# One attention and two MLP layers on one core: layer 1's first tokens loaded during attention, two of its buffers in space of their own, three buffers for raw weights

## The chip, the cores and the metric

The kernel runs on one core of a Trainium2 chip. The metric is device microseconds of one execution; the median of three runs of the kernel before is 1123.8 us (1122.57 to 1123.87). The engines are named as in the profile: PE is TensorE (PEld its weight loads), DVE VectorE, ACT ScalarE, POOL GpSimd, SP the queue that issues all DMAs here.

## The reference

Attention with a threshold (scores more than tau below the row's maximum are dropped), then two MLP layers, all in float32:

```python
scores = q @ k.T * scale                       # 4 batches, 8 heads, 576 tokens, head width 64
scores = where(scores >= max - tau, scores, -1e9)
x  = softmax(scores) @ v                       # gathered to 2304 tokens x 512
h  = x @ w_in1;  x = (h * sigmoid(1.702 * h)) @ w_out1      # 512 -> 2048 -> 512
h  = x @ w_in2;  out = (h * tanh(softplus(h))) @ w_out2     # 512 -> 2048 -> 512
```

The weights reach the kernel as 64-bit words of which the kernel makes float32 values itself (called conversion below), and every matrix product of the MLP layers is done in three passes, with each operand split in a high and a low part.

## The kernel before

Three stages follow each other on PE: attention, layer 1, layer 2. Activations pass between them through DRAM (`x_d`).

**Attention** runs over 80 groups (4 batches, 4 pairs of heads, 5 tiles of query rows). A group is: scores on PE (L586), the softmax on DVE (L605, L609, L615), ACT (L612) and POOL (L628), transposes on PE (L662) with copies on ACT (L672), the product with v on PE (L683), and a copy on ACT (L691). When a pair of heads is done its rows are stored to `x_d` (L693). Score banks and the four banks of `h` in layer 1 share PSUM: layer 1's first matmul must come after the last scores (`open_hb`).

**Layer 1** runs over five blocks of tokens (512, 256, 512, 512, 512) and, in each, over 16 slices `f` of the hidden width. `h1(j, f)` is 12 matmuls (L487), a tanh (L513, ACT), a product (L516, DVE), a copy to the high part `gh` (L518, ACT) and the difference `gl` (L519, DVE). `o1(j, f)` is 12 matmuls (L532) that accumulate the output; it comes two units behind, so that PE's order is h(n), o(n-2), h(n+1), and so on.

**Weights.** Slice `f` has 1 MB of raw words (two loads, L368 and L372) in a buffer of the ring `sr` (`NSR` buffers). `conv_w` makes a value of them in a buffer of the ring `sv` (three buffers): ACT L377 and L379, DVE L383 and L386, POOL L389, DVE L391. `split_w` makes the high part (ACT L397) and the low part (DVE L399) in the slice's own space. Slice f is allowed to start when group 60 + 4f has its softmax; from f=5 on that is the last group. Layer 2's weights are converted in layer 1's second block and after (`stage_w2`) and go through DRAM.

**Tokens.** `load_x(layer, j, rank)` brings a block's tokens in two halves: a load into an `sv` buffer (L468), a copy to the high part on ACT (L472), the difference on DVE (L474). Block 0 goes to `xa`, a tile that exists from the start. Rings hand out their buffers in the order in which the program calls them.

**Order.** Nothing is executed in the order of the text: `Order` keeps a list of operations with engine, duration, what they depend on and a rank, and a greedy planner at build time writes out each engine's queue. An engine that comes free takes the ready operation of lowest rank. A load is put down as 2.0 us and its bytes at 200e3 per us, one after the other (`DMA_US`, `DMA_RATE`). Operations with `port=True` (the conversion's on DVE and POOL, L474, L615, L628) are never planned at the same time on DVE and POOL. On the chip each queue then runs in that order, each instruction waiting for what it needs.

`opened` stands for the end of attention: only then `a`, attention's pool, is closed, and its space is used for weights 12 to 15, `x`, and layer 1's `t`, `gh`, `gl` and `x2`.

Of the kernel before, what the change touches and what calls it, by code (L numbers as in the profile page):

```python
# [22 lines left out]
PR = 2  # L23
AR = 0.1
NORM_P = 1.0
NSR = 2
NSV = 3
WARM = 1
FG = 0.2
# [14 lines left out]
C0 = 60  # L44
C1 = 4
D0 = 16
D1 = 2


class Order:  # L50
# [23 lines left out]
    def add(self, eng, dur, fn, r=(), w=(), rank=0.0, deps=(), nbytes=None, port=False, steps=1):  # L74
        n = len(self.ops)
        if port:
            self.port.add(n)
        before = set(deps)
        for key in r:
            if key in self.writer:  # L80
                before.add(self.writer[key])
        for key in w:
            if key in self.writer:
                before.add(self.writer[key])
            before.update(self.readers.get(key, ()))
        for key in r:
            self.readers.setdefault(key, []).append(n)
        for key in w:
            self.writer[key] = n
            self.readers[key] = []  # L90
        before.discard(n)
        self.ops.append((eng, dur, fn, before, rank, nbytes, steps))
        return n
# [106 lines left out]
def attention_then_two_ffn_kernel(  # L200
# [98 lines left out]
    def t_mm(n, k=1):  # L299
        return k * (max(n, 256) * 0.4167e-3 + 0.0125)  # L300

    def t_dve(n, fast=False):
        return 0.065 + n * (0.52e-3 if fast else 1.042e-3)

    def t_act(n, ptr=0, psum=True):
        return (0.05 if psum else 0.09) + n * 0.833e-3 + 0.093 * ptr
# [7 lines left out]
    def dma(fn, nbytes, r=(), w=(), rank=0.0, deps=(), dur=0.47):  # L314
        return add("SP", dur, fn, r, w, rank, deps, nbytes)
# [14 lines left out]
    spool = stage_ctx.enter_context(tc.tile_pool(name="s", bufs=1, side="right"))  # L330
    srs = Ring(spool, "sr", NSR, [128, 4 * DM], F32)
    svs = Ring(vpool, "sv", NSV, [128, 2 * DM], F32)
    W = []

    def make_w(pool, upto):
        for f in range(len(W), upto):
            W.append([pool.tile([128, 2 * DM], F32R, name=f"w{p}{f}") for p in "hl"])
# [64 lines left out]
    def load_w1(f, rank, deps):  # L402
        val, kval = conv_w(1, f, rank, deps)
        split_w(f, val, kval, rank)
# [9 lines left out]
    def load_w2(f, rank):  # L414
# [5 lines left out]
    late = {  # L420
        "x": LateRing("x", 1, [128, 2, KD, T], F32R),
        "o": LateRing("o", NOUT, [128, 512], F32),
        "x2": LateRing("x2", 4, [128, T], F32),
        "t": LateRing("t", 2, [128, T], F32),
        "gh": LateRing("gh", 3, [128, T], F32R),
        "gl": LateRing("gl", 3, [128, T], F32R),
        "m": LateRing("ms", 5, [128, T], F32),
        "hs": LateRing("hs", NHS, [128, T], F32),
        "g2h": LateRing("g2h", NG2, [128, T], F32R),
        "g2l": LateRing("g2l", NG2, [128, T], F32R),  # L430
    }

    def open_late(olds, new):

        def go():
            for old in olds:
                old.close()
            if len(W) < KF:
                make_w(ctx.enter_context(tc.tile_pool(name="wb", bufs=1)), KF)
            for where, name, rings, side in new:  # L440
                pool = where.enter_context(tc.tile_pool(name=name, bufs=1, side=side))
                for ring in rings:
                    late[ring].make(pool)

        return go
# [7 lines left out]
    def load_x(layer, j, rank):  # L453

        t0, n = blocks[layer][j]
        deps = [i for i, lay, a, b in x_stores if lay == layer and a < t0 + n and b > t0]
        x, kx = (lambda: x0), ("xa", 0)
        if x_n[0] % 2:
            x, kx = late["x"].next()
            deps.append(opened)  # L460
        x_n[0] += 1
        keys = []
        for i in range(2):
            rt, kr = svs.next()
            r = rt.rearrange("p (c t) -> p c t", c=2)[:, :, 0:n]
            cs = slice(2 * i, 2 * i + 2)
            kh, kl = kx + (0, i), kx + (1, i)
            dma(lambda r=r, cs=cs: nc.sync.dma_start(  # L468
                out=r, in_=x_d[layer][cs, :, t0:t0 + n].rearrange("c p t -> p c t")),
                256 * n * 4, [], [kr], rank, deps)  # L470
            add("ACT", t_act(2 * n, psum=False),
                lambda r=r, cs=cs: nc.scalar.copy(x()[:, 0, cs, 0:n], r), [kr], [kh], rank, deps)  # L472
            add("DVE", t_dve(2 * n),
                lambda r=r, cs=cs: nc.vector.tensor_tensor(  # L474
                    x()[:, 1, cs, 0:n], r, x()[:, 0, cs, 0:n], ALU.subtract),
                [kr, kh], [kl], rank, port=True)
            keys += [kh, kl]
        xt[layer, j] = (x, keys)

    def mm_h(dst, layer, j, f):  # L480
        n = blocks[layer][j][1]
        ih, il = (parts(w)[0] for w in W[f])
        x = xt[layer, j][0]()
        i = 0
        for c in range(KD):
            for a, lo in ((ih, 0), (ih, 1), (il, 0)):
                nc.tensor.matmul(  # L487
                    hb[dst][:, 0:n], a[:, c, :], x[:, lo, c, 0:n], start=(i == 0), stop=(i == 3 * KD - 1))
                i += 1
                yield  # L490
# [9 lines left out]
    def h1(j, f, rank):  # L500

        n = blocks[1][j][1]
        i, kb = hbanks[len(steps) % 4]
        steps.append(add("PE", t_mm(n, 3 * KD) + 0.05, lambda: mm_h(i, 1, j, f),
            xt[1, j][1] + [("wh", f), ("wl", f)], [kb], rank, outs[-1:] + [open_hb], steps=3 * KD))
        t, kt = late["t"].next()
        gh, kgh = late["gh"].next()
        gl, kgl = late["gl"].next()

        def h():  # L510
            return hb[i][:, 0:n]

        add("ACT", t_act(n), lambda: nc.scalar.activation(t()[:, 0:n], h(), AF.Tanh, scale=0.851),  # L513
            [kb], [kt], -1.0, [opened])
        add("DVE", t_dve(n),
            lambda: nc.vector.scalar_tensor_tensor(h(), t()[:, 0:n], 1.0, h(), ALU.add, ALU.mult),  # L516
            [kt], [kb], -1.0)
        add("ACT", t_act(n), lambda: nc.scalar.copy(gh()[:, 0:n], h()), [kb], [kgh], -1.0)  # L518
        add("DVE", t_dve(n), lambda: nc.vector.tensor_tensor(gl()[:, 0:n], h(), gh()[:, 0:n], ALU.subtract),  # L519
            [kb, kgh], [kgl], -1.0)  # L520
        gt[j, f] = (gh, gl, [kgh, kgl])
# [201 lines left out]
    att, marks, behind, scored = [], [], [], []  # L723
# [14 lines left out]
    def load_w1_from(fs):  # L738
        for f in fs:
            load_w1(f, BIG / 2 + f, [marks[min(C0 + C1 * f, len(marks) - 1)]])  # L740

    early = (len(marks) - 1 - C0) // C1 + 1
    load_w1_from(range(early))
    load_x(1, 0, len(marks) - 12)
    open_hb = add("SP", 0.0, open_h, deps=scored, rank=-10.0)
    l1_ctx = ExitStack()
    opened = add("SP", 0.0, open_late([att_ctx], [
        (ctx, "x", ("x",), "left"),
        (l1_ctx, "l1", ("t", "gh", "gl", "x2"), "left"),
    ]), deps=att, rank=-10.0)  # L750

    load_w1_from(range(early, KF))
# [4 lines left out]
    for n in range(n1 + 2):  # L757
        if n < n1:
            j, f = divmod(n, KF)
            h1(j, f, BIG + n)  # L760
            if f == 2 and j + 1 < NB:
                load_x(1, j + 1, -0.5)
            f, r = divmod(n - D0, D1)
            if 0 <= f < KF and not r:
                stage_w2(f, BIG / 2 + 100 + f, [steps[n]])
        if n >= 2:
            o1(*divmod(n - 2, KF), BIG + n)
    l1 = outs + [i for i, *_ in x_stores]


    G = 2
    NG = KF // G
    opened2 = add("SP", 0.0, open_late([l1_ctx, stage_ctx], [
        (ctx, "l2", ("m", "hs", "o"), "left"), (ctx, "g2", ("g2h", "g2l"), "right"),
    ]), deps=l1 + staged, rank=-10.0)
# [154 lines left out]
```

## Time and profile before

| | |
|---|---|
| median of 3 runs | 1123.8 us |
| the profiled execution | 1123.02 us, span 1121.2 us |
| PE busy | 1087.8 us (97%) |
| DVE, ACT, POOL busy | 700.8, 659.1, 211.4 us |
| granted TensorE clock | 0.989 of full, mean |
| attention's last matmul | at 311.3 us |
| layer 1's first matmul | at 312.7 us |
| first matmul of f=15 in block 0 | at 410.7 us |

The span is from the first to the last instruction of the trace; the 1.8 us between it and the execution's time lie around it. Busy time of an engine counts overlapping instructions once. PE is busy nearly throughout, so what matters is the short stretches in which it isn't, and those in which its clock is granted at half.

### The profile page before, as it was taken

What the parts mean: (1) busy time and instruction counts of PE and PEld (TensorE: products, weight loads), DVE (VectorE), ACT (ScalarE), POOL (GpSimd) and SP (SyncE); (2) the same over time, 40 slices, a digit from 0 to 9 for tenths busy, and PEclk for the clock granted to TensorE, in tenths of its full rate; (3) what the DMA queues carried; (4) which work ended last, traced back from release to release, by engine and by line L of the source; (5) the groups of instructions that cost most, each with busy time, mean ns of one, the idle gap of its engine ahead of it and who ended that gap; (6) DMA issues with size and microseconds to landing.
All of it is one profiled execution on the core that took longest, in us unless ns stands there. A gap on an engine that the chain in (4) does not pass through costs nothing.

```text
span 1121.2 us, 17713 instructions
## 1 busy us (share of the span) xinstructions
PE 1087.8 (97%) x6757; PEld 888.0 (79%) x6757; DVE 700.8 (63%) x1540; ACT 659.1 (59%) x1065; POOL 211.4 (19%) x182
## 2 busy tenths in 40 slices
PE   9999999999759999999999999999999999999998
PEld 7677777777548879988888888888888888888887
DVE  6988888899867665555542344465655554464554
ACT  4677777778656564444532344577565655646665
POOL 3444343456622312222110000000000000000000
PEclk9999999999869999999999999999999999999999
DMA  2122121423344345564540123420010010010010
GB/s 87 48 86 71 62 88 45 125 82 106 105 142 151 113 144 175 188 208 168 185 154 1 56 95 99 130 73 1 29 38 1 10 38 1 1 38 0 1 38 19
DMA packets 44165, 89.75 MB, mean 80 GB/s; under 512 B 3376, under 2 KB 21296, under 8 KB 44080
## 3 DMA queue, kind: packets, MB, share of 16 engines
q1 hardware_dynamic: 44080, 88.62, 24.0%
q8 instruction: 53, 0.87, 0.3%
q14 instruction: 32, 0.26, 0.1%
HBM read 66.06 MB, written 22.54 MB: 79 GB/s over the span
## 4 chain that ended last, share of the span: by engine, by line
PE 82%; DVE 8%; ACT 3%; POOL 2%; issue 2%; POOLq 0%; ACTq 0%; DVEq 0%
PE h L487 32%; PE tb L849 17%; PE tb L532 14%; PE tb L683 6%; PE sc L586 6%; PE tb L662 6%; POOL sv L389 2%; DVE p L615 2%; DVE ss L605 2%; DVE sv L391 1%; DVE wl L399 1%; ACT wh L397 1%; DVE sv L386 1%; DVE sv L383 1%; ACT p L612 0%
## 5 line engine op out<-in xcount | busy, mean ns | idle before, releaser
L487 PE MATMUL h<-xa,wh 128*128 128x512 f32 x640 | 200.7, 395 | 11.2 <-ACT xa L472 7.9
L811 ACT ACTIVATE ms<-ms 128x512 f32<-128x512 f32 (+1 forms) x240 | 131.1, 583 | 133.4 <-DVE ms L796 132.4
L487 PE MATMUL h<-x,wh 128*128 128x512 f32 (+1 forms) x640 | 165.2, 346 | 0.0
L628 POOL TENSOR_SCALAR p<-p,sm 128x576 f32<-128x576 f32 x144 | 132.5, 934 | 164.0 <-DVE sm L623 108.2
L487 PEld LDWEIGHTS h<-xa,wh 128*128 128x128 f32 x640 | 121.5, 190 | 38.2 <-ACT xa L472 8.8
L612 ACT ACTIVATE p<-ss,nm 128x576 f32<-128x576 f32 x144 | 112.0, 781 | 58.9 <-DVE ss L605 50.1
L605 DVE TENSOR_SCALAR_CACHE_REDUCE ss<-sc,nqsc 128x576 f32<-128x576 f32 x144 | 112.4, 813 | 30.8 <-PE sc L586 30.6
L513 ACT ACTIVATE t<-h 128x512 f32<-128x512 f32 (+1 forms) x80 | 44.4, 555 | 142.6 <-PE h L487 142.3
L487 PE MATMUL h<-xa,wl 128*128 128x512 f32 x320 | 126.1, 394 | 0.5 <-DVE wl L399 0.5
L821 DVE TENSOR_TENSOR ms<-ms,hs 128x512 f32<-128x512 f32 (+1 forms) x80 | 50.1, 636 | 122.1 <-ACT ms L811 122.0
L487 PEld LDWEIGHTS h<-x,wh 128*128 128x128 f32 x640 | 112.6, 189 | 15.7
L615 DVE SCALAR_TENSOR_TENSOR p<-ss,nm,p 128x577 f32<-128x577 f32 x144 | 123.3, 887 | 2.4 <-POOL p L628 1.1
L532 PE MATMUL tb<-gl,wh 128*128 128x512 f32 (+1 forms) x320 | 117.9, 369 | 1.1 <-DVE gl L519 1.1
L516 DVE SCALAR_TENSOR_TENSOR h<-t,h 128x512 f32<-128x512 f32 (+1 forms) x80 | 51.2, 642 | 107.9 <-ACT t L513 107.7
L532 PE MATMUL tb<-gh,wh 128*128 128x512 f32 (+1 forms) x320 | 117.7, 368 | 0.0
L532 PE MATMUL tb<-gh,wl 128*128 128x512 f32 (+1 forms) x320 | 117.7, 368 | 0.0
L389 POOL TENSOR_TENSOR sv<-sv,sr 128x1024 uint32<-128x1024 uint32 x32 | 78.3, 2447 | 194.9 <-DVE sv L386 162.3
L849 PE MATMUL tb<-wh,g2h 128*128 128x512 f32 x288 | 112.1, 389 | 0.0
L849 PE MATMUL tb<-wl,g2h 128*128 128x512 f32 x288 | 112.1, 389 | 0.0
L849 PE MATMUL tb<-wh,g2l 128*128 128x512 f32 x288 | 112.0, 389 | 0.0
L487 PE MATMUL h<-x,wl 128*128 128x512 f32 (+1 forms) x320 | 110.9, 347 | 0.0
L586 PE MATMUL sc<-kq 64*128 64x288 f32 (+1 forms) x640 | 101.2, 428 | 3.1 <-DVE ss L605 3.0
(55 smaller groups left out, 1761.3 us busy)
## 6 DMA issues: line engine op xcount, KB each, us to landing
sr<-in_w_in SPq DMA_DIRECT2D x32, 512.0 KB, 4.5
sr<-in_w_out SPq DMA_DIRECT2D x32, 512.0 KB, 5.4
kq<-in_kq SPq DMA_DIRECT2D x16, 576.0 KB, 3.8
sv<-x_d SPq DMA_DIRECT2D x16, 512.0 KB, 4.5
w_d<-sv SPq DMA_DIRECT2D x16, 512.0 KB, 3.0
sv<-w_d SPq DMA_DIRECT2D x16, 512.0 KB, 3.3
vr<-in_v SPq DMA_DIRECT2D x16, 320.0 KB, 4.4
x_d<-xo SPq DMA_DIRECT2D x16, 288.0 KB, 4.7
```

What stands on the lines that cost most here:

```text
L389: lambda: nc.gpsimd.tensor_tensor(bits, bits, word(0), ALU.add), keys, [kval], rank, port=True)
L487: nc.tensor.matmul(hb[dst][:, 0:n], a[:, c, :], x[:, lo, c, 0:n], start=(i == 0), stop=(i == 3 * KD - 1))
L532: nc.tensor.matmul(accs[e][0][:, 0:n], a[:, es], b()[:, 0:n], start=(f == 0 and i == 0), stop=(f == KF - 1 and i == 2), skip_group_check=True,
L586: nc.tensor.matmul(dst, q, kq2[rows, n * SH:(n + 1) * SH], start=True, stop=True)
L605: lambda: nc.vector.tensor_scalar(n3, s3, nqsc, None, ALU.mult, ALU.min, accum_out=nm[:, 0:1]),
L612: lambda: nc.scalar.activation(p[:, 0:S], ns[:, 0:S], AF.Exp, bias=nm[:, 0:1], scale=-1.0),
L615: lambda: nc.vector.scalar_tensor_tensor(p, ns, nm[:, 1:2], p, ALU.is_le, ALU.mult, accum_out=sums[:, col:col + 1]),
L628: lambda p=p, r=r: nc.gpsimd.tensor_scalar(p[:, 0:S], p[:, 0:S], r, 0.0, ALU.mult, ALU.add),
L662: nc.tensor.transpose(tb[bank][0:rows, c0 + i * 128:c0 + (i + 1) * 128], p[:, k0:k0 + rows], ident)
L683: nc.tensor.matmul(av[64 * i:64 * i + 64], vr[0:rows, c, 64 * i:64 * i + 64], pn[0:rows, c0 + i * w:c0 + (i + 1) * w], start=(n == 0), sto ...
L811: nc.scalar.activation(m()[:, 0:n], m()[:, 0:n], fn, bias=bias)
L849: nc.tensor.matmul(accs[t][0], x[:, t * 128:(t + 1) * 128], w, start=(f == 0 and i == 0), stop=(f == KF - 1 and i == 2), skip_group_check= ...
```

## The change

The load of layer 1's block 0 gets rank 40 and is called before the weights' loads, so that it takes the first two `sv` buffers and comes as soon as batch 0 is stored. `t`, `gh` and `gl` get a pool of their own on the right side, made at the start, and the tanh no longer depends on `opened`. The ring of raw words has three buffers. `x2` stays in the pool that is made when attention is closed.

```diff
-NSR = 2
+NSR = 3
...
+XR = 40
...
+    l1_ctx = ExitStack()
+    l1pool = l1_ctx.enter_context(tc.tile_pool(name="l1e", bufs=1, side="right"))
+    for ring in ("t", "gh", "gl"):
+        late[ring].make(l1pool)
+
...
         add("ACT", t_act(n), lambda: nc.scalar.activation(t()[:, 0:n], h(), AF.Tanh, scale=0.851),
-            [kb], [kt], -1.0, [opened])
+            [kb], [kt], -1.0)
...
     early = (len(marks) - 1 - C0) // C1 + 1
+    load_x(1, 0, XR)
     load_w1_from(range(early))
-    load_x(1, 0, len(marks) - 12)
     open_hb = add("SP", 0.0, open_h, deps=scored, rank=-10.0)
-    l1_ctx = ExitStack()
     opened = add("SP", 0.0, open_late([att_ctx], [
         (ctx, "x", ("x",), "left"),
-        (l1_ctx, "l1", ("t", "gh", "gl", "x2"), "left"),
+        (l1_ctx, "l1", ("x2",), "left"),
     ]), deps=att, rank=-10.0)
```

## Rows read from the trace of the kernel before

**Rows 1.** Waits of PE from 20 us on: total us, times, longest us.

```profile
PE h L487 <- ACT xa L472: 7.9, 2, 6.6
...
PE tb L532 <- DVE gl L519: 1.1, 2, 0.6
PE h L487 <- DVE wl L399: 0.5, 1, 0.5
```

**Rows 2.** Timeline of PE: start, us, instruction, count, idle before and its releaser.

```profile
304.28 1.98 PE L683 MATMUL tb<-pm,vr 128*64 128x128 f32 x16 [4.28 <-ACT pm L672]
...
310.92 0.40 PE L683 MATMUL tb<-pmt,vr 96*64 96x64 f32 x8
...
326.29 0.80 PE L487 MATMUL h<-xa,wh 128*128 128x512 f32 x1 [2.31 <-DVE xa L474]
...
410.68 0.62 PE L487 MATMUL h<-xa,wh 128*128 128x512 f32 x2
```

**Rows 3.** The chain that ended last, a unit of matmuls in layer 1.

```profile
474.04 2.72 PE h L487 x12
```

**Rows 4.** The same chain: one turn of the conversion from f=8, and f=15.

```profile
347.58 2.42 POOL sv L389
...
350.03 1.24 DVE sv L391
...
351.29 1.06 ACT wh L397
...
352.38 1.23 DVE wl L399
353.61 0.61 DVE h L516
354.21 0.61 DVE sv L383
...
354.84 0.70 DVE sv L386
...
403.70 2.44 POOL sv L389
```

**Rows 5.** Timeline of DVE: a split of x, a product, the last weight's low part.

```profile
323.16 3.07 DVE L474 TENSOR_TENSOR xa<-sv,xa 128x1024 fp32r<-128x1024 f32 x1 [0.54 <-ACT xa L472]
...
333.42 0.70 DVE L516 SCALAR_TENSOR_TENSOR h<-t,h 128x512 f32<-128x512 f32 x1 [1.35 <-ACT t L513]
...
408.51 1.22 DVE L399 TENSOR_TENSOR wl<-sv,wh 128x1024 fp32r<-128x1024 f32 x1
```

**Rows 6.** Windows: length, busy us (instructions) of PE, PEld, DVE, ACT, POOL, granted clock, DMA.

```profile
160.00:180.00 20.00, 19.64 (x211) 14.48 (x207) 17.41 (x57) 15.36 (x32) 7.50 (x10) 1.00 0.22 63
...
320.00:330.00 10.00, 4.51 (x10) 3.26 (x11) 8.04 (x8) 6.71 (x7) 2.79 (x2) 0.50 0.36 116
330.00:340.00 10.00, 10.00 (x43) 8.20 (x42) 7.41 (x10) 5.86 (x9) 2.46 (x2) 0.94 0.48 173
```

**Rows 7.** Timeline of POOL, the additions of slices f=3 to f=7.

```profile
305.49 2.39 POOL L389 TENSOR_TENSOR sv<-sv,sr 128x1024 uint32<-128x1024 uint32 x1
314.02 2.40 POOL L389 TENSOR_TENSOR sv<-sv,sr 128x1024 uint32<-128x1024 uint32 x1 [6.15 <-ACT sr L379]
322.76 2.39 POOL L389 TENSOR_TENSOR sv<-sv,sr 128x1024 uint32<-128x1024 uint32 x1 [6.34 <-DMA sr<-in_w_out]
329.61 2.51 POOL L389 TENSOR_TENSOR sv<-sv,sr 128x1024 uint32<-128x1024 uint32 x1 [4.45 <-ACT sr L379]
339.65 2.44 POOL L389 TENSOR_TENSOR sv<-sv,sr 128x1024 uint32<-128x1024 uint32 x1 [7.54 <-DVE sv L386]
```

**Rows 8.** The page's DMA issues: count, KB each, median us to landing.

```profile
sr<-in_w_in SPq DMA_DIRECT2D x32, 512.0 KB, 4.5
```

**Rows 9.** Timelines of SP and ACT: raw words of f=8 loaded, their conversion begun.

```profile
335.27 0.37 SPq L368 DMA_DIRECT2D sr<-in_w_in  x1
...
344.75 1.14 ACT L377 ACTIVATE sv<-sr 128x1024 f32<-128x1024 f32 x1
```

## The prediction

> **What bounds the kernel now.** I read the waits of PE first. Behind the start there is one large one: layer 1's first matmuls waited 7.9 us for the copies of block 0's tokens [rows 1]. PE's timeline shows it in place: attention's last matmul ends at 311.3, and only from 326.29 on, after another 2.31 us for the tokens' low parts, does PE run through; before that, from 300.0 to 304.28, it stood 4.28 us for a copy that ACT had to do [rows 2]. From 326.29 on PE does a unit of 12 matmuls in 2.72 us [rows 3] and waits only 1.6 us more, 1.1 for `gl` and 0.5 for a weight [rows 1].
>
> So the tokens look like the bound. The chain that ended last says otherwise: from 347.58 to 403.70 it runs not through PE but through the conversion of the weights, POOL, DVE, ACT and DVE in turn, (403.70 - 347.58)/7 = 8.02 us for each of the slices f=8 to f=15 [rows 4]. The last low part (f=15) ends at 408.51 + 1.22 = 409.73 [rows 5], and PE starts on it at 410.68, when the unit in front of it is done [rows 2]. PE's late start and the slow weights thus meet within a microsecond: whatever is won on one alone is lost on the other. From 410.68 on PE is the bound, and the change adds nothing there. The place to watch is the start of h(0,15), now at 410.68.
>
> **Tokens early.** Two loads, two copies and two differences leave the stretch between attention and layer 1 and go into attention, some 25 groups in. In such a stretch DVE has 20 - 17.41 = 2.6 us free in 20 and ACT 4.6 [rows 6]. The work is two ACT copies of about 1.06 us (L397 has the same size [rows 4]) and two DVE differences of between 1.23 (L399, the same form and size [rows 4]) and 3.07 (the one at 323.16, while POOL worked from 322.76 to 325.15 [rows 5, 7]). DVE's part is 2.5 to 6.1 us against 2.6 free in 20: from nothing to 3.5 us of attention. I take nothing, since a list planner starts them where DVE is idle and 2.5 nearly fits one such window; without that cover it is 2.5. On SP the two loads stand behind the store that they read, so the queue is held for about a transfer's landing (4.5 us for a load of that size [rows 8]); behind them are the loads of the next pair of heads, whose two buffers put them nearly a pair ahead of their use. Nothing is charged.
>
> With tokens there, PE follows attention directly. Its floor: h(0,15) has 15 h units and 13 o units in front of it, 28 x 2.72 = 76.2 us, so 311.3 + 76.2 = 387.5; if h units also fill the hole of 4.28, 383.2. It could start 23 to 27 us earlier if the weights were there.
>
> **Space of their own for `t`, `gh`, `gl`.** The tanh no longer waits for `opened`. The four score banks allow four h units, 10.9 us of PE, before a tanh is needed at all, so the old condition would have held PE little; no instruction is added. I price it at nothing in either direction.
>
> **Three raw buffers.** This decides. In the turn that starts with f=8 the steps stand one behind the other: 2.42 (L389), 1.24 (L391), 1.06 (L397), 1.23 (L399), 0.61 (a product of layer 1), and for f=9 0.61 (L383) and 0.70 (L386) [rows 4]. Why are the last two behind L399 of f=8? The raw words of f=8 were issued at 335.27 [rows 9] and land in about 4.5 us [rows 8], by 341 with the second load; L377 begins on them only at 344.75 [rows 9]. The words were there and the queue was not: it was written so. The kernel's planner books 8.2 us for two loads (two issues, 2.0, twice 2.62), and with the conversion behind them a raw buffer's round is some 15.6 by its constants, 7.8 per slice with two buffers. The trace's 8.0 is that order, carried out. With three buffers the same round gives 5.2 and no longer spaces the slices; next comes the planner's rule that marked work on DVE and POOL never overlaps.
>
> Then DVE can do L383 and L386 of the next slice while ACT does L397. Its 1.06 leaves the turn: 8.02 - 1.06 = 6.96; if layer 1's product goes under L389 instead of standing in the turn, 6.35. The trace has one turn with the next words in place and its own delays: from f=5 to f=6, 329.61 - 322.76 = 6.85 [rows 7]. I take 6.85. Bounds: below, the steps on DVE and POOL alone, 2.42 + 1.24 + 1.23 + 0.61 + 0.70 = 6.2; above, the old average, (403.70 - 305.49)/12 = 8.2 [rows 4, 7].
>
> A rule of the notes bears on the lower bound. The rows: a difference took 3.07 us while POOL worked, against 1.23 [rows 4, 5, 7]. The Trainium skill, GPSIMD Engine Reference, section Specifications, says that GpSimd shares its SBUF interfaces with VectorE and contends with VectorE's instructions of two SBUF inputs; the trace agrees. It speaks against a larger gain: were both free to overlap, DVE's 3.8 us of conversion and 1.4 of layer 1 per slice would fit under PE's 5.44, and PE's floor would set the time, 1095.5 to 1099.8.
>
> **The sum.** Attention fills DVE and POOL until f=3 adds, which stays at 305.49. The words of f=4 now lie ready, whose addition today waits 6.15 us for ACT's part [rows 7]. It comes at 305.49 + 2.39 + 1.24 + (0.61 + 0.70) + 1.23 = 311.7 instead of 314.02. Eleven turns of 6.85 lead to the addition of f=15 at 387.0; from there to its low part it is today 409.73 - 403.70 = 6.0 [rows 4, 5]. So h(0,15) starts at 393.0, later than PE's floor of 387.5 (or 390, if PE's first units run at half clock). The gain is 410.68 - 393.0 = 17.7 us. The profiled execution took 1123.02, 0.8 below the median of the three runs; 1123.02 - 17.7 = 1105.3.
>
> **Rivals.** (A) *The conversion's order stays.* For it: no engine waited for the words of f=8. Against: the turn of 6.85. Eleven turns of 8.1 give 311.7 + 89.1 + 6.0 = 406.8, a gain of 3.9: 1119.1.
>
> (B) *The weights come early enough and PE's floor decides*, from a turn of (387.5 - 6.0 - 311.7)/11 = 6.3 down. For it: the bound of 6.2. Against: layer 1's two DVE operations a slice (0.7 for the product [rows 5]) have no place outside the turn but L389's 2.4. h(0,15) starts at 383.2 to 390: 1095.5 to 1102.3.
>
> (C) *Slower: the conversion is caught behind layer 1 in DVE's queue.* With weights as the bound, PE's h(n) starts when slice n is ready, and its tanh and product follow. If L391 of a later slice stands behind that product, as it did at 333.42, where the product waited 1.35 for the tanh [rows 5], conversion and PE take turns. That turn, f=6 to f=7, took 339.65 - 329.61 = 10.04 [rows 7]. Eleven of them: 311.7 + 110.4 + 6.0 = 428.1, 17.4 us later than now: 1140.4. It decides from (410.68 - 6.0 - 311.7)/11 = 8.5 a turn. Against: it is one turn in twelve.
>
> (D) *The clock.* At 6.85 a slice PE idles 6.85 - 5.44 = 1.4 in each. After its long wait PE's clock was granted at 0.50 in the window 320 to 330 and 0.94 in the next [rows 6], so at half rate (1.2 GHz) from 326.29 to about 331.2: 2.4 us lost. Paid in all 15 slices, 36 us, h(0,15) starts at 387.5 + 36 = 423.5: 1135.8, slower. It limits itself, since a PE that is late has no gaps. The Trainium skill, TensorE: Matmul & The Clock Gate, section HAM oscillation, tells of a kernel whose matmul groups start slow after every wait for data; here one long wait shows it, and no row shows gaps of 1.4.
>
> **How the numbers follow.** My forecast has 0.68, A 0.14, B 0.10, C 0.05, D 0.03. A measurement of this kernel can tell some 0.2% (2.2 us) from no change. Of A, 0.11 lies above that and 0.03 within. Faster: 0.68 + 0.10 + 0.11 = 0.89; same 0.03; slower 0.08. The forecast's own range, turns of 6.3 to 7.3, is 387 to 398 for h(0,15), 1099 to 1110. For 8 in 10 I go to 1097 (into B) and 1118 (into A, a little short of its centre); the far half of A, C and D stay outside.
>
> **What the profile will show.** Right: PE's first h units within 2 us of attention's end or among its last groups, with no wait for `xa`; L389 every 6.7 to 7 us from 312 on; L383 and L386 of the next slice between L391 and L399; waits of PE of about 1.4 us a slice; h(0,15) near 393; nothing changed behind it. Wrong: turns of 8 us or more, a DVE wait for a tanh in front of L391, attention's end past 315, or half clock in block 0.

## The result, and the profile after

The changed kernel takes 1104.26 us (median of 4 runs, 1103.53 to 1104.98) against 1123.18 beside it: a ratio of 0.9833, 95% interval 0.9816 to 0.985. The profiled execution took 1103.53, 19.5 less than the one shown of before. Lines moved: the conversion's and the split's numbers are higher by one (L390 is the addition on POOL, L400 the low part), those of `load_x` and behind by five or six (L493 is h, L538 is o, L519 the tanh, L522 the product, L678 attention's copies on ACT).

The page of the changed kernel, its first lines:

```profile
span 1101.7 us, 17703 instructions
## 1 busy us (share of the span) xinstructions
PE 1081.4 (98%) x6757; PEld 883.6 (80%) x6757; DVE 709.7 (64%) x1540; ACT 658.7 (60%) x1065; POOL 219.6 (20%) x182
```

PE's waits from 20 us on (total us, times, longest us), the three that answer to [rows 1] and to the hole at 300:

```profile
PE tb L689 <- ACT pm L678: 2.1, 3, 1.6
...
PE tb L538 <- DVE gl L525: 0.3, 1, 0.3
PE h L493 <- DVE wl L400: 0.3, 1, 0.3
```

The 7.9 us for the tokens and the hole of 4.28 are gone. PE's timeline of the same kernel, then three rows of before:

```profile
288.02 1.30 PE L668 MATMUL tb<-ident,p 128*128 128x128 f32 x5 [1.33 <-ACT pm L678]
...
296.39 1.19 PE L592 MATMUL sc<-kq 64*64 64x288 f32 x8
...
298.69 0.73 PE L493 MATMUL h<-xa,wh 128*128 128x512 f32 x2
...
315.73 0.57 PE L689 MATMUL tb<-pm,vr 128*64 128x64 f32 x12 [1.56 <-ACT pm L678]
316.12 0.41 PE L689 MATMUL tb<-pmt,vr 96*64 96x64 f32 x8
316.46 0.50 PE L538 MATMUL tb<-gh,wh 128*128 128x512 f32 x1
...
388.62 0.61 PE L493 MATMUL h<-xa,wh 128*128 128x512 f32 x2
389.51 0.50 PE L493 MATMUL h<-xa,wl 128*128 128x512 f32 x1 [0.28 <-DVE wl L400]
...
401.69 0.28 PE L538 MATMUL tb<-gh,wh 128*128 128x256 f32 x1
```

```profile
293.69 1.19 PE L586 MATMUL sc<-kq 64*64 64x288 f32 x8
...
335.33 0.39 PE L532 MATMUL tb<-gh,wh 128*128 128x512 f32 x1
...
421.17 0.28 PE L532 MATMUL tb<-gh,wh 128*128 128x256 f32 x1
```

The first h unit starts at 298.69, 2.3 us behind attention's last scores and among its last transposes. Three h units lie inside attention, which ends at 316.5; the first o unit follows at once. Compare attention's end and the first matmul without gaps in [rows 2]. I measure all kernels at one mark, the first o unit of the second block: 421.17 before, 401.69 after. The difference is 19.48, that of the spans 19.5: all is decided ahead of the mark, and nothing changed behind it. Nearly all of it is the earlier first o unit (335.33 before, 316.46 after: 18.87); from there to the mark PE takes 85.2 us instead of 85.8. So the faster weights shorten no stretch; they let PE keep the earlier start.

The additions of f=3, f=4, f=10 and f=15 on POOL, against [rows 7] and the last line of [rows 4]:

```profile
305.16 2.44 POOL L390 TENSOR_TENSOR sv<-sv,sr 128x1024 uint32<-128x1024 uint32 x1 [0.81 <-DVE sv L387]
311.23 2.41 POOL L390 TENSOR_TENSOR sv<-sv,sr 128x1024 uint32<-128x1024 uint32 x1 [3.62 <-DVE sv L387]
...
350.23 3.31 POOL L390 TENSOR_TENSOR sv<-sv,sr 128x1024 uint32<-128x1024 uint32 x1 [2.73 <-DVE sv L387]
...
382.07 2.82 POOL L390 TENSOR_TENSOR sv<-sv,sr 128x1024 uint32<-128x1024 uint32 x1 [3.20 <-DVE sv L387]
```

Eleven turns from f=4 to f=15 take 382.07 - 311.23 = 70.8, 6.44 each instead of 8.0. One turn on DVE, and the last low part, of the same kernel:

```profile
347.54 1.23 DVE L392 SCALAR_TENSOR_TENSOR sv<-sr,sv 128x1024 uint32<-128x1024 uint32 x1 [0.38 <-POOL sv L390]
348.68 0.69 DVE L384 TENSOR_SCALAR sv<-sv 128x1024 f32<-128x1024 f32 x1
349.41 0.69 DVE L387 TENSOR_SCALAR sv<-sv 128x1024 uint32<-128x1024 uint32 x1
350.02 1.22 DVE L400 TENSOR_TENSOR wl<-sv,wh 128x1024 fp32r<-128x1024 f32 x1
351.15 0.69 DVE L522 SCALAR_TENSOR_TENSOR h<-t,h 128x512 f32<-128x512 f32 x1
352.49 0.69 DVE L525 TENSOR_TENSOR gl<-h,gh 128x512 fp32r<-128x512 f32 x1 [0.66 <-ACT gh L524]
...
388.23 1.23 DVE L400 TENSOR_TENSOR wl<-sv,wh 128x1024 fp32r<-128x1024 f32 x1 [1.12 <-ACT wh L398]
```

L384 and L387 of the next slice now stand right behind L392 and ahead of L400, as the prediction said. In [rows 4] they came behind L399. The new turn is still shorter than forecast. Layer 1's product L522 (351.15) stands beside the addition instead of in the turn. The addition itself starts at 350.23, while L400 runs from 350.02 to 351.24; it takes 3.31 then instead of 2.44, so that this overlap saves little: the two take 3.52 us together, and one behind the other they would take 1.22 + 2.44 = 3.66.

### The profile page after: what moved, and what is told of

Read it like the earlier page. It is cut to its first block, busy times and chain, and to the rows that moved or that the text cites. A ratio compares the mean times of both kernels' runs of the same rounds, so it can differ in the third digit from the quotient of the medians.

```text
span 1101.7 us, 17703 instructions
## 1 busy us (share of the span) xinstructions
PE 1081.4 (98%) x6757; PEld 883.6 (80%) x6757; DVE 709.7 (64%) x1540; ACT 658.7 (60%) x1065; POOL 219.6 (20%) x182
## 4 chain that ended last, share of the span: by engine, by line
PE 85%; DVE 7%; ACT 2%; issue 1%; POOL 1%; ACTq 0%; POOLq 0%; DVEq 0%
PE h L493 35%; PE tb L854 18%; PE tb L538 16%; PE tb L689 6%; PE tb L668 6%; PE sc L592 5%; DVE p L621 2%; DVE ss L611 2%; ACT p L618 1%; POOL sv L390 1%; DVE wl L400 1%; DVE sv L392 1%; DVE sv L384 0%; ACT xo L697 0%; DVE sv L387 0%
## 5 line engine op out<-in xcount | busy, mean ns | idle before, releaser
L493 PE MATMUL h<-xa,wh 128*128 128x512 f32 x640 | 197.4, 390 | 0.0
L493 PE MATMUL h<-x,wh 128*128 128x512 f32 (+1 forms) x640 | 165.3, 347 | 0.0
L493 PEld LDWEIGHTS h<-xa,wh 128*128 128x128 f32 x640 | 119.8, 188 | 24.7
L519 ACT ACTIVATE t<-h 128x512 f32<-128x512 f32 (+1 forms) x80 | 44.5, 556 | 138.9 <-PE h L493 138.4
L493 PEld LDWEIGHTS h<-x,wh 128*128 128x128 f32 x640 | 112.7, 189 | 15.8
L493 PE MATMUL h<-xa,wl 128*128 128x512 f32 x320 | 124.8, 390 | 0.4 <-DVE wl L400 0.3
L522 DVE SCALAR_TENSOR_TENSOR h<-t,h 128x512 f32<-128x512 f32 (+1 forms) x80 | 51.3, 641 | 112.4 <-ACT t L519 112.1
L390 POOL TENSOR_TENSOR sv<-sv,sr 128x1024 uint32<-128x1024 uint32 x32 | 85.6, 2678 | 163.7 <-DVE sv L387 134.3
L538 PE MATMUL tb<-gl,wh 128*128 128x512 f32 (+1 forms) x320 | 117.8, 368 | 0.3 <-DVE gl L525 0.3
L538 PE MATMUL tb<-gh,wh 128*128 128x512 f32 (+1 forms) x320 | 117.9, 368 | 0.0
L538 PE MATMUL tb<-gh,wl 128*128 128x512 f32 (+1 forms) x320 | 117.7, 368 | 0.0
L493 PE MATMUL h<-x,wl 128*128 128x512 f32 (+1 forms) x320 | 110.9, 347 | 0.0
```

What stands on the lines that cost most here:

```text
L390: lambda: nc.gpsimd.tensor_tensor(bits, bits, word(0), ALU.add), keys, [kval], rank, port=True)
L493: nc.tensor.matmul(hb[dst][:, 0:n], a[:, c, :], x[:, lo, c, 0:n], start=(i == 0), stop=(i == 3 * KD - 1))
L538: nc.tensor.matmul(accs[e][0][:, 0:n], a[:, es], b()[:, 0:n], start=(f == 0 and i == 0), stop=(f == KF - 1 and i == 2), skip_group_check=True,
```

## The experiments

Theory: the order that the planner wrote for two raw buffers spaced the slices, PE's late start and the slow weights met within a microsecond, so that only the parts together win. Rivals: one of the two is the bound alone; the third buffer holds words that were really late.

**e1, two raw buffers.**

```diff
-NSR = 3
+NSR = 2
```

> The changed kernel with two raw buffers instead of three. Theory (the ring of raw words, as the planner books it, spaces the slices): additions about 8.0 us apart in layer 1's first block, the last low part near 405 us, PE waiting for weights by then, 1117 to 1120 us. Rival (the late tokens alone were the bound, the third buffer is idle): additions stay near 6.4 us, 1104 to 1106 us.

1122.64 us, ratio 0.9997 (0.9987 to 1.0006). All the tokens' gain is gone. In its timelines (POOL, then PE), with the clock of one window:

```profile
313.45 2.41 POOL L390 TENSOR_TENSOR sv<-sv,sr 128x1024 uint32<-128x1024 uint32 x1 [4.14 <-ACT sr L380]
...
402.51 2.42 POOL L390 TENSOR_TENSOR sv<-sv,sr 128x1024 uint32<-128x1024 uint32 x1 [6.56 <-DVE sv L387]
```

```profile
357.69 1.14 PE L493 MATMUL h<-xa,wh 128*128 128x512 f32 x2 [2.69 <-ACT wh L398]
...
373.75 0.73 PE L493 MATMUL h<-xa,wh 128*128 128x512 f32 x2 [2.47 <-ACT wh L398]
```

```profile
370.00:380.00 10.00, 7.00 (x23) 5.06 (x22) 5.14 (x7) 4.83 (x6) 3.78 (x2) 0.83 0.29 105
```

Turns are 8.1, f=15 adds at 402.51 (403.70 before). PE starts early, then waits for slices, up to 2.69 at once, and its clock falls in such windows (0.83 here). The rival is out. The theory expected 3 to 6 us and got 0 to 2 (its mark is at 419.33): f=4 added at 313.45 and not at the 311.7 of the forecast, and PE, waiting for slices and at times at half clock, used up its earlier start.

**e2, three raw buffers alone.** In the kernel before:

```diff
-NSR = 2
+NSR = 3
```

> The kernel before with three raw buffers and nothing else. Theory (late tokens and slow weights meet within a microsecond): slices ready earlier, PE still starts near 326 us and can win only the 1.6 us of waits behind that, 1121 to 1123 us. Rival (the weights alone were the bound): about 1105 us.

1118.91 us, 0.9968 (0.9956 to 0.998): 3.6 us, more than the 1.6 expected and far from 1105. PE's timeline:

```profile
322.64 0.80 PE L487 MATMUL h<-xa,wh 128*128 128x512 f32 x1 [8.61 <-ACT xa L472]
324.32 0.79 PE L487 MATMUL h<-xa,wh 128*128 128x512 f32 x1 [0.88 <-DVE xa L474]
```

The tokens still come late, but PE runs through from 324.32 instead of 326.29 [rows 2], 2.0 us, and the 1.6 of later waits are gone. (The profiled executions differ by 4.6. The listed idle time understates a wait: in the trace of before one of 0.63 at 408.05 sets two matmuls 1.02 us apart instead of 0.23.) The low part of f=15 starts 13 us earlier (395.40 against 408.51 [rows 5]) and nobody uses that. Without the third buffer the change is worth 0 us, the third buffer alone is worth 4, together 19.

**e3, two raw buffers and a planner that books loads faster.** In the changed kernel:

```diff
-DMA_RATE = 200e3
+DMA_RATE = 400e3
-NSR = 3
+NSR = 2
```

> The changed kernel with two raw buffers, and with loads booked by the planner at 400e3 bytes per us instead of 200e3, so that a buffer's round is some 13.0 by its constants instead of 15.6. Nothing in the hardware changes; only the order written out does. Theory (the order spaces the slices, the words themselves come early): turns of 6.5 to 7.0 us, 1104 to 1109 us. Rival (the words of a third buffer are really needed in time): turns stay near 8 us, 1117 to 1120 us.

1107.49 us, 0.9863 (0.9849 to 0.9878): 15.2 us less than e1, with two buffers too. Between e1 and e3 nothing differs but a number that the planner reads. On POOL, then one row of ACT:

```profile
313.60 2.44 POOL L390 TENSOR_TENSOR sv<-sv,sr 128x1024 uint32<-128x1024 uint32 x1 [11.29 <-ACT gh L524]
...
387.15 2.46 POOL L390 TENSOR_TENSOR sv<-sv,sr 128x1024 uint32<-128x1024 uint32 x1 [4.62 <-ACT sr L380]
```

```profile
337.03 1.16 ACT L378 ACTIVATE sv<-sr 128x1024 f32<-128x1024 f32 x1 [3.14 <-DMA sr<-in_w_out]
```

Turns are 6.7 from f=4 on. The new order moved attention as well (its last scores come at 289.55, 4.2 us earlier than in e1), but f=4 adds at the same time as in e1 (313.60 and 313.45) and f=15 15.4 us earlier: the turns made the gain. So it was the order. Words do come late now at times (ACT waits 3.14 for a load): two buffers are tight in this order, but a third is worth 1.7 us there (e10; the two intervals overlap), not 18.

**e4 and e9, the tanh held until attention's end.** e4 has `t`, `gh`, `gl` in the late pool and the old dependency; e9 has them in their own space and only the dependency.

```diff
-            [kb], [kt], -1.0)
+            [kb], [kt], -1.0, [opened])
```

and in e4 alone

```diff
-    for ring in ("t", "gh", "gl"):
-        late[ring].make(l1pool)
...
-        (l1_ctx, "l1", ("x2",), "left"),
+        (l1_ctx, "l1", ("t", "gh", "gl", "x2"), "left"),
```

> The changed kernel, but with t, gh and gl in the pool that is made when attention is closed, and the tanh planned behind that, as in the kernel before. Theory (four score banks hold four h units, so PE has work until then): within 3 us of the changed kernel, 1104 to 1107 us. Rival (the space of their own is what lets layer 1 start inside attention): h units leave attention's last groups, 8 us lost there, 1110 to 1114 us.

> The changed kernel, t, gh and gl in their own space, with one difference: the tanh is still planned behind the end of attention. It tells the two halves of that part apart. Theory A (the order holds the tanh back: the planner puts the end of attention behind its last store, and weight work in ACT's queue comes before): as with the old space, PE stands about 14 us before the first o unit, 1116 to 1119 us. Theory B (it is the shared space, whose last users on the chip must be done first): like the changed kernel, 1103 to 1106 us.

1117.89 (0.9955, 0.9939 to 0.9972) and 1117.43 (0.995, 0.9935 to 0.9965). I was wrong on e4 by 11 us, and its rival by 4; of e9's theories A was right. PE in e4, its ACT, and PE in e9 (in e4 the lines of layer 1 are five lower: L514 is the tanh, L519 the copy to `gh`, L533 o):

```profile
330.50 0.79 PE L533 MATMUL tb<-gh,wh 128*128 128x512 f32 x1 [13.96 <-ACT gh L519]
```

```profile
323.57 1.05 ACT L398 CAST wh<-sv 128x1024 fp32r<-128x1024 f32 x1 [2.44 <-DVE sv L392]
324.52 1.13 ACT L378 ACTIVATE sv<-sr 128x1024 f32<-128x1024 f32 x1
325.55 1.11 ACT L380 ACTIVATE sr<-sr 128x1024 f32<-128x1024 uint32 x1
326.57 1.06 ACT L514 ACTIVATE t<-h 128x512 f32<-128x512 f32 x2
```

```profile
330.98 0.80 PE L538 MATMUL tb<-gh,wh 128*128 128x512 f32 x1 [13.97 <-ACT gh L524]
```

The three h units lie inside attention in e4 too. Behind them PE's order has the first o unit, which needs a `gh`, and only then the fourth h unit (o at 330.50, h at 335.40); so nothing was left for PE when attention ended, and it stood 14 us for the first `gh`. The tanh came at 326.57 behind three steps of weights in ACT's queue. e9 does the same with space of its own: the order holds the tanh back, not the shared space.

**e5 and e6, weights spread over attention.**

```diff
-C0 = 60
-C1 = 4
+C0 = 20
+C1 = 10
```

(e6: 40 and 6.)

> The changed kernel with slice f allowed from group 20 + 10f instead of 60 + 4f: six slices lie inside attention, spread out. Theory (in the changed kernel PE and the weights meet again, so taking the weights away leaves only PE's own waits and the crowded end of attention): weights early, PE without a gap from attention on, 1099 to 1103 us. Rival (attention has no room, each slice moved into it makes it longer by about its 3.9 us on DVE): attention's last scores 6 to 10 us later, 1105 to 1112 us.

> The changed kernel with slice f allowed from group 40 + 6f: seven slices allowed inside attention, closer together than from 20 + 10f. Theory: as with 20 + 10f, but with two or three slices left over at attention's crowded end, 1100 to 1104 us. Rival (no room in attention): 1105 to 1112 us.

1105.8 (0.9851, 0.9837 to 0.9864) and 1105.47 (0.9847, 0.9833 to 0.986), not better than the changed kernel. A window of e5:

```profile
80.00:200.00 120.00, 113.29 (x1173) 84.88 (x1169) 116.48 (x329) 92.80 (x189) 68.92 (x60) 1.00 0.31 98
```

PE is busy for 113.3 us there, 117.3 in the changed kernel. Neither e5 nor e6 waits for a weight in layer 1, yet last scores come at 297.36 and 301.43 instead of 296.39, and the first o unit at 320.49 and 320.68 instead of 316.46. Attention pays some 4 us for the slices moved into it, less than the rival's 6 to 10. What early weights give back is smaller: from the first o unit to the mark PE takes 83.4 us in both, against 85.2 in the changed kernel.

**e7, the clamp left out** for layer 1's weights, one DVE step of 0.69 per slice.

```diff
+        if layer == 2:
-        add("DVE", t_dve(n, True),
+            add("DVE", t_dve(n, True),
...
```

> The changed kernel without the clamp (L384) of layer 1's weights, so that each slice has one DVE step of 0.69 us less; the values of weights out of the clamp's range are not mended. Theory (PE and weights meet within a microsecond in layer 1's first block): turns of 5.6 to 5.9 us, the last low part 6 us earlier, but the time only 1 to 2.5 us lower, 1102 to 1103.5 us. Rival (the weights alone are the bound): 11 turns times 0.6, 1097 to 1098.5 us.

1100.85 us, 0.9804 (0.9791 to 0.9817): 3.4 below the changed kernel, between the theory's 1 to 2.5 and the rival's 6 to 7. POOL's additions of f=4 and f=15, then PE's first o unit and the mark:

```profile
307.66 3.30 POOL L391 TENSOR_TENSOR sv<-sv,sr 128x1024 uint32<-128x1024 uint32 x1 [0.69 <-ACT t L520]
...
372.73 2.43 POOL L391 TENSOR_TENSOR sv<-sv,sr 128x1024 uint32<-128x1024 uint32 x1 [3.56 <-DVE sv L388]
```

```profile
315.70 0.50 PE L539 MATMUL tb<-gh,wh 128*128 128x512 f32 x1
...
399.06 0.28 PE L539 MATMUL tb<-gh,wh 128*128 128x256 f32 x1
```

f=15 adds 9.3 us earlier, the mark comes 2.6 earlier. PE waits for no weight here. The first o unit comes 0.8 earlier, with attention's end; from there to the mark PE takes 83.4 us, as in e5 and e6, instead of 85.2. So late weights, with its one wait for a `gl`, hold the changed kernel by 1.9 us at most; then PE is the bound.

**e8, f=3 and f=4 not before attention's end.**

```diff
-            load_w1(f, BIG / 2 + f, [marks[min(C0 + C1 * f, len(marks) - 1)]])
+            load_w1(f, BIG / 2 + f, [marks[C0 + C1 * f if f < 3 else -1]])
```

> The changed kernel with slices f=3 and f=4 allowed only behind the last group's softmax, like those from f=5 on; their words can then not be converted among attention's last groups. Theory (with three raw buffers the first ACT step of f=3 stands before a copy of attention's and holds PE, and the last scores come 2.7 us late): last scores back at about 293.7 us, the weights 1 to 3 us later, the time within 1.5 us of the changed kernel either way. Rival (the late scores come from the tokens or from h units in between): last scores stay near 296.4 us.

1114.15 us, 0.992 (0.9905 to 0.9934). PE, then POOL's addition of f=4, which is 9.2 us later than in the changed kernel:

```profile
294.17 1.19 PE L592 MATMUL sc<-kq 64*64 64x288 f32 x8
```

```profile
320.46 3.31 POOL L390 TENSOR_TENSOR sv<-sv,sr 128x1024 uint32<-128x1024 uint32 x1 [2.72 <-DVE sv L387]
```

The last scores come 2.2 us earlier, as expected. But its turns are as short, 6.3, and 9.2 us of lateness at f=4 cost 8 (profiled executions) to 10 us (medians). The weights' start counts nearly in full. I had put that at 1 to 3, and the time within 1.5 us.

**e10 and e11, three buffers and loads booked at 400e3 and 300e3.**

```diff
-DMA_RATE = 200e3
+DMA_RATE = 400e3
```

(e11: 300e3.)

> The changed kernel with loads booked at 400e3 bytes per us. With two buffers that order brought attention's last scores at 289.55 us, 6.8 us earlier than in the changed kernel, and lost it to weights that PE waited 6.3 us for. Theory (PE's floor, attention's end with the h units inside it, sets the time where weights are early enough): with a third buffer the weights follow, 1098 to 1102 us. Rival (what attention gains the weights lose, whatever the number of buffers): 1104 to 1108 us.

> The changed kernel with loads booked at 300e3 bytes per us, between the two. Theory (PE's floor decides): between 1098 and 1104 us, with attention's last scores between 289.5 and 296.4 us. Rival (attention and weights take turns): 1104 to 1108 us.

1105.79 (0.9846, 0.9832 to 0.9861) and 1109.1 (0.9876, 0.986 to 0.9893). PE's waits in e10:

```profile
PE h L493 <- DVE wl L400: 8.2, 9, 2.1
```

Its last scores come at 286.98, 9.4 us earlier than in the changed kernel, and PE waits 8.2 us for weights that come as late as there (f=15 adds at 383.10, against 382.07). The rival was right: what attention gains, PE loses to the weights. e11 is worse than both neighbours and outside both of its ranges; attention's copies held PE once for 3.4 us. No order tried that does all of the work beats the changed kernel.

## Why the prediction was right, point by point

**The time.** 1105.3 forecast, 1104.26 measured; a gain of 17.7 against 19.5 in the profiled executions. That it is so near is in part luck: see h(0,15).

**What bounds.** That tokens and weights meet within a microsecond is shown by e1 and e2: 0 us without the third buffer, 3.6 by the third buffer alone, 18.9 together. No run has the third buffer and the early tanh with late tokens; e2's wait of 8.61 for the tokens would stand in front of PE there too.

**Tokens early, nothing.** Right: e1's last scores come at 293.77, 0.1 from those of before (293.69). The two differences took 1.22 and 1.68 on DVE, at 107 and 115 us.

**Space of their own, nothing in either direction.** Wrong, the step that failed. It is worth some 13 us once tokens are early (e4 and e9 against the changed kernel). The step counted four h units, 10.9 us of PE, in front of the first tanh that PE needs; by the order h(n), o(n-2) it is three, and it took PE to have them still to do at the end of attention, where it had done all three. And it didn't ask where in ACT's queue the planner would put a tanh that waits for attention's last store: behind weights. What does it is the tanh's early place in the order, which e9 takes away alone; the space of its own makes that place possible. It cost the forecast nothing, since the sum went on with the tanh free.

**Three raw buffers: the order, not the words.** Right, by e3. The forecast of the order was right in its parts (f=4 at 311.7, measured 311.23; L384 and L387 ahead of L400). The turn was mis-sized: 6.85 forecast, 6.44 measured, near the 6.35 that the prediction gave for a turn with layer 1's product under the addition, where that product now stands (351.15). L400 and the next addition overlap (350.02 and 350.23), which the prediction took to be excluded by the planner's rule: the rule holds in the plan, and the chip's queues did not keep to it. By the 3.52 against 3.66 us above that is worth little.

**h(0,15) at 393.0.** It started at 388.62, 4.4 us before the forecast and 22.1 earlier than in the kernel before: f=15 added at 382.07 instead of 387.0, and from there it took 6.6 us instead of 6.0. Only 19.5 of the 22.1 reached the time. PE's trace has 15 o units in front of h(0,15) before and 14 after, where the prediction's floor counted 13; so one o unit, 2.72 us, moved behind it. The forecast was late at this place and counted all of it as gain, and the two errors nearly cancel. The start lies in the range of rival B, PE's floor, as well as in the forecast's own, and B's mechanism is as near as the forecast's: e7 takes the weights 9.3 us forward and wins 3.4, and late weights cost PE 1.9 us at most. B's time, up to 1102.3, was missed by the o unit that moved. The last low part ends at 389.46; PE, which wants it there, waits 0.28. The waits of 1.4 a slice that the forecast named as a sign did not appear. PE came to slices late (h(0,3) at 319.31, 14.2 us after f=3 was added), and the slices, 6.44 apart against PE's 5.44, only used up that lead: at f=15 6.6 us were left (382.07 to 388.62), and the steps behind the addition need 7.4.

**Attention's end past 315** was named as a sign of error and came (316.5). That is 5.2 us later than before. Of these 2.5 lie behind the last scores, where attention now holds three h units (8.8 us) and no longer the hole of 4.28; the other 2.7 are a late arrival of the last scores, 296.39 against 293.69, which the prediction missed. With a third buffer f=3 has its words early, and its first step stands ahead of a copy that PE needs. ACT in the changed kernel, and the same copy before:

```profile
286.27 1.13 ACT L378 ACTIVATE sv<-sr 128x1024 f32<-128x1024 f32 x1
287.30 1.05 ACT L678 COPY pm<-tb 128x512 f32<-128x512 f32 x2
```

```profile
286.45 1.05 ACT L672 COPY pm<-tb 128x512 f32<-128x512 f32 x2
```

The copy is 0.85 us late by it; the second step (L380, 288.51) stands ahead of the next copies, and how the 2.7 divide between the two isn't shown. e8 takes both steps away and the scores come back; e1 and e2 put it down to the third buffer (293.77 and 296.16).

**Rivals C and D** did not come in the changed kernel: DVE had L392 behind a product (341.05, 341.65) without a wait for it, and the mean granted clock is 0.998 against 0.989. The mechanism of D is real: e1 shows it with waits near 2.5 us.

## What to carry to other kernels

When a stage starts late for one reason, look at what would have been late next, in place: here the last weight was ready 0.95 us before PE wanted it, so the change without the third buffer won nothing, the third buffer alone 4 us, and together 19 us. Where queues are written by a planner, ask of each serial chain whether an engine waited for data or only for its turn; here a buffer, or one constant of the planner, was worth nearly the same. A dependency that doesn't bind now binds once the wait in front of it is gone: price it in the changed kernel, not in this one (the tanh, priced at nothing, held 13 of the 19 us).

## What the runs showed of the hardware that was not expected

Where a POOL addition and a DVE instruction of the weights overlap in these rows, the one that starts first keeps its time. L400, begun 0.21 us ahead of the addition, keeps its 1.22 us and the addition takes 3.31 instead of 2.44. Begun behind the addition, DVE waits it out. Two cases in the changed kernel, a clamp (0.69 alone) and a split (1.22 alone) on DVE:

```profile
358.50 2.33 DVE L384 TENSOR_SCALAR sv<-sv 128x1024 f32<-128x1024 f32 x1
...
383.14 2.85 DVE L400 TENSOR_TENSOR wl<-sv,wh 128x1024 fp32r<-128x1024 f32 x1
```

The additions beside them began at 356.99 and 382.07 and ended at 360.29 and 384.89, 0.54 and 1.10 us before the two. The product L522, whose output and one input (`h`) lie in PSUM, keeps its 0.69 beside an addition (351.15).

A wait of 2.41 us in e8 and one of 2.06 in e10 left PE's clock at full, while e1's waits of 2.47 and 2.69, one every 16 us, brought windows at 0.83 and 0.89; no run here separates their length from what lies between them.
